# Batch 0's queries in the quadrant layout, with the head's and the units' steps in a new order: pooled attention and an MLP mixer on one core

## The chip, the core and the metric

One core of a Trainium2 chip. The time is device microseconds of one launch; the median of three runs of the kernel before is 266.4 us (266.19 to 267.63). A profile of one execution, with every instruction's start and duration and every DMA packet, stands beside the times. PE is the matrix engine (TensorE), PEld its weight loads, DVE the vector engine, ACT the scalar engine, POOL GpSimd, SP SyncE.

## What is computed

For 8 batches, 8 heads, 576 rows and head dimension 64, keys and values are averaged over groups of 8 rows (72 pooled keys), attention is taken against them, and the result goes through two MLPs, one over rows, one over channels:

```python
k_p = k.reshape(B, H, 72, 8, 64).mean(axis=3); v_p = v.reshape(B, H, 72, 8, 64).mean(axis=3)
attn = softmax(q @ k_p.T / 8)                    # 576 x 72 for each batch and head
x = (attn @ v_p), heads side by side             # 576 x 512 for each batch
h = relu(x.T @ w_tok1) @ w_tok2                  # w_tok1 576 x 256, w_tok2 256 x 576
u = x + h.T
out = u + relu(u @ w_ch1) @ w_ch2                # w_ch1 512 x 1536, w_ch2 1536 x 512
```

## The kernel before

**Units.** The channel MLP makes the bulk of the work. It runs as nine units, one for each batch's first 512 rows and a last one for all batches' remaining rows. A unit (`unit_fast`) is twelve first-layer tiles (`l1_tile`, L517: four 128x512 matmuls each, then a ReLU on ACT, L521) and seven products of the second layer (`product`, L583), which work on sums and differences of halves that DVE makes (`g_sums`, L545 and L557). A unit yields after every half tile; at each yield index the table `PLAN[n]` names the steps of other batches that are issued there. So while unit n runs, the attention of batch n+1 is done between its matmuls, and loads and poolings of batches further ahead.

**Steps.** `b.lk`, `b.lq`, `b.lv` load a batch's keys, queries, values (POOL issues these DMAs, which also cast to bf16). `b.K0`, `b.K1`, `b.V0`, `b.V1` pool the keys or values of four heads on POOL (three adds, L174, L175, then L178 or L180); a small letter (`2.v1`) puts the same on DVE; `kpool`, `vpool` do it on PE with eight identity matmuls (L253, L264). `kpT` transposes pooled keys on PE (L222) and ACT copies them to `kD`. `Q0`, `Q1` (`qD`, L284) transpose queries on DVE in 32x32 blocks of pairs, so that four heads stand in four quadrants of 32 partitions. `s0` to `s2` (`scores`, L297) multiply quadrant by quadrant (each matmul uses 32 rows of the array, the four heads four different ones) and ACT takes the exponential (L306). `av` (L379) multiplies with the values, DVE divides (L383, L384); `at` (L393) and `u` (L415) are the row MLP; `t` (L424) transposes the sum on PE; for batches 3 to 7 `M` and `T` do that by way of DRAM and DVE. `=1` to `=4` are `g_sums`, `w0` to `w3` (`weight_sum`) the same for weights, once. `g` is a gate: a one-element write on DVE and a read of it on POOL (L712, L713), which holds POOL until DVE has come that far.

**The order.** Inside `manual_schedule` every engine's instructions stand in the order in which the program issues them. Loads by POOL go through one queue in issue order, with eight transfers outstanding: issue n waits until transfer n-8 has landed.

**The head.** Before unit 0, the string `HEAD` lists the steps of batch 0, which has routes of its own. `LkA`, `LkB`, `LkT` load its keys in three parts (heads 0 to 3 and 4 to 7 of rows' groups 0 to 63, then groups 64 to 71 of all heads); `LvA`, `LvB`, `LvT` the same of values; `Lq` half the queries, the other half comes by two SP loads in fp32 that `c0` (ACT) and `c1` (DVE) cast (L690). `Lt1`, `Lt2`, `Lc1a` to `Lc1d`, `Lc2a` to `Lc2c` load weights, `Lk1`, `Lq1`, `Lv1` batch 1. `dN` issues N matmuls on a zeroed tile (L679, `warm`), whose result nobody reads. `q0` to `q3` (`qT`, L275) transpose pairs of heads on PE, five 128x128 blocks each, and DVE copies them (L277). `kp0` to `kp2` pool the keys on PE (L232), DVE copies into `kpz`, which has zeroes beside each head; `kt0` to `kt2` (L243) transpose that so that even and odd rows of queries have each a zero-padded key tile `kT`. `o0` to `o3`, `e0` to `e3` (`score`, L318) are eight scores of two heads each, every one with one exponential on ACT (L322). `a00` to `a14` (`avh`, L333), `m00` to `m14` (`ath`, L356), `X0` to `X3` and `A0` to `A3` (`uT_x`, L468; `uT_a`, L476) are the rest of attention and the row MLP for four heads at a time; `p0`, `p1` reorder `w_tok2` on ACT and POOL (L159). Score tiles and `a` tiles share two double banks of PSUM in turn (`ps_two`); other products take turns in four single banks.

Of the kernel before, what the change touches and what calls it, by code (L numbers as in the profile page):

```python
# [20 lines left out]
HEAD = """LkA LkT LkB LvT Lq LvA LvB Lt1 Lk1 Lt2 Lc1b Lc1a Lq1 Lc1c Lv1 Lc1d p1 Lc2a Lc2b Lc2c d2 d2 d3 d1 d4 d4 c0 c1 prep q0 kp0 kp1 kt0 q1 d1 o0 kt1 kp2 e0 e1 q3 kt2 o1 q2 e3 vpool0 o3 e2 a00 vpool1 a02 o2 m01 d1 d1 m00 a04 X1 m03 a14 m02 X0 m04 p0 a10 a12 1.kpool m10 m14 m12 m13 m11 A1 A0 X2 X3 A2 A3"""  # L21
PLAN = [
# [13 lines left out]
def kernel(  # L36
# [21 lines left out]
    NE = (BR + 1) // 2  # L58
    EV, OD = NE * BP, (BR - NE) * BP
# [43 lines left out]
    kpz = area[0:SP, 0:1536].rearrange("j (h e d) -> j h e d", h=H, e=3)  # L103
    kT = area[:, 2048:2048 + 2 * H * SP].rearrange("m (o k) -> m o k", o=2)
    qT0 = area[:, 3200:3200 + 2 * HP * EV].rearrange("m (a l n) -> m a l n", a=HP, l=2)
# [30 lines left out]
    def q_pairs(a0, a1):  # L136
        return q[0, 2 * a0:2 * a1].rearrange("(a l) (p r) d -> (l p) a (r d)", l=2, r=BR)
# [49 lines left out]
    def batch_steps(b):  # L187
# [5 lines left out]
        def prepare():  # L193
            kp = att.tile([SP, 2, 2, 4, D // 2], BF16, name="kp") if b >= 1 else None
            st.update(kp=kp, vp=values[par], ex=exps[par], xt=rests[b // 2 % 2])
            if not first:
                st["kD"] = att.tile([P, 2, 2, SP], BF16, name="kD")
# [29 lines left out]
        def kp2(h0, h1):  # L227
            def go():
                ps = take([P, 512], FP32)
                n = (h1 - h0) * D  # L230
                for i in range(POOL):
                    nc.tensor.matmul(out=ps[0:SP, 0:n], lhsT=ident[0:SP, 0:SP], rhs=loaded[b, "k"][:, h0:h1, i, :],  # L232
                                     start=(i == 0), stop=(i == POOL - 1))
                nc.vector.tensor_copy(out=kpz[:, h0:h1, 1, :], in_=ps[0:SP, 0:n].rearrange("j (h d) -> j h d", d=D))
                give(ps)
            return go

        def kt2(h0, h1):
            def go():
                ps = take([P, 2, h1 - h0, SP], BF16)  # L240
                for odd in range(2):
                    for h in range(h0, h1):
                        nc.tensor.transpose(out=ps[:, odd, h - h0, :],  # L243
                                            in_=kpz[:, h, 1 - odd:3 - odd].rearrange("j e d -> j (e d)"),
                                            identity=ident[0:SP, 0:SP])
                nc.vector.tensor_copy(out=kT[:, :, h0 * SP:h1 * SP], in_=ps.rearrange("m o h j -> m o (h j)"))
                give(ps)
            return go
# [22 lines left out]
        def qT(hp):  # L271
            def go():
                ps = take([P, NE, 2, BP], BF16)
                for rr in range(NE):
                    nc.tensor.transpose(out=ps[:, rr].rearrange("m l p -> m (l p)"),  # L275
                                        in_=loaded[b, "q"][:, hp, rr * P:(rr + 1) * P], identity=ident)
                nc.vector.tensor_copy(out=qT0[:, hp].rearrange("m l (r p) -> m r l p", p=BP), in_=ps)  # L277
                give(ps)
            return go

# [8 lines left out]
        def scores(i):  # L289
            def go():  # L290
                pss = [ps_two.tile([P, 2, 512], FP32, name="p2") for _ in range(2)]
                spans = [(i, 0, 0, S1)] if i < 2 else [(g, g * (S - S1), S1, S) for g in range(2)]
                for g, o, n0, n1 in spans:
                    for db in range(2):
                        for l in range(4):
                            quad = slice(l * 32, (l + 1) * 32)
                            nc.tensor.matmul(out=pss[l // 2][0:SP, l % 2, o:o + n1 - n0], lhsT=st["kD"][quad, g, db, :],  # L297
                                             rhs=st["qD"][quad, g, n0:n1, db], start=(db == 0 and o == 0),
                                             stop=(db == 1), tile_position=(l * 32, 0), skip_group_check=True)
                exv = st["ex"][:, 0:H * S].rearrange("j (g a l n) -> j a l g n", g=2, a=2, l=2)  # L300
                for a in range(2):
                    if i < 2:
                        dst, src = exv[:, a, :, i, 0:S1], pss[a][0:SP, :, 0:S1]
                    else:
                        dst, src = exv[:, a, :, :, S1:S], pss[a][0:SP, :, 0:2 * (S - S1)].rearrange("j l (g n) -> j l g n", g=2)
                    nc.scalar.activation(out=dst, in_=src, func=AF.Exp, scale=scale)  # L306
            return go

        def score(hp, odd):
            n = OD if odd else EV  # L310

            def go():
                ps = ps_two.tile([P, 2, 512], FP32, name="p2")
                exv = st["ex"][:, 0:H * S].rearrange("j (h n) -> j h n", h=H)[:, 2 * hp:2 * hp + 2]
                for hl in range(2):
                    h = 2 * hp + hl
                    keys = slice(h * SP, (h + 1) * SP)
                    nc.tensor.matmul(out=ps[0:SP, hl, 0:n], lhsT=kT[:, odd, keys], rhs=qT0[:, hp, hl, 0:n],  # L318
                                     start=True, stop=True)
                dst = exv.rearrange("j h (r p) -> j h r p", p=BP)[:, :, odd:BR:2, :]  # L320
# [462 lines left out]
```

## Time and profile before

| | |
|---|---|
| median of three runs | 266.4 us (266.19, 266.4, 267.63) |
| span of the profiled execution | 264.4 us, from first to last instruction; the runs' median is 2.0 us longer |
| PE busy | 256.2 us (97%), 2121 matmuls |
| DVE, ACT, POOL busy | 178.4 us (67%), 119.6 us (45%), 153.1 us (58%) |
| PE's first matmul, first key matmul, first L517 | 1.19, 8.04 and 24.60 us |
| DMA rate from 16 to 57.5 us | 199 to 206 GB/s |

PE's longest waits by the list of waits are 1.3 us for the first keys and 0.9 us for pooled keys of batch 2 (at 57 us); everything else is under half a microsecond. From about 15 us on the matmuls follow one another almost without a hole.

### The profile page before, as it was taken

What the parts mean: (1) busy time and instruction counts of PE and PEld (TensorE: products, weight loads), DVE (VectorE), ACT (ScalarE), POOL (GpSimd) and SP (SyncE); (2) the same over time, 40 slices, a digit from 0 to 9 for tenths busy, and PEclk for the clock granted to TensorE, in tenths of its full rate; (3) what the DMA queues carried; (4) which work ended last, traced back from release to release, by engine and by line L of the source; (5) the groups of instructions that cost most, each with busy time, mean ns of one, the idle gap of its engine ahead of it and who ended that gap; (6) DMA issues with size and microseconds to landing.
All of it is one profiled execution on the core that took longest, in us unless ns stands there. A gap on an engine that the chain in (4) does not pass through costs nothing.

```text
span 264.4 us, 5328 instructions
## 1 busy us (share of the span) xinstructions
PE 256.2 (97%) x2121; PEld 160.3 (61%) x2121; DVE 178.4 (67%) x370; ACT 119.6 (45%) x195; POOL 153.1 (58%) x177
## 2 busy tenths in 40 slices
PE   8799999989999999999999999999999999999994
PEld 3685466744677545774487447744874486486483
DVE  3557569996787655895599678844795576184183
ACT  2355763149536456425641575165435412612700
POOL 8577326899999999988959982898200010100000
PEclk9999999999999999999999999999999999999999
DMA  6999999993088928699447940830513053404104
GB/s 141 193 195 206 205 207 208 205 216 80 4 129 141 166 82 171 149 202 266 91 132 107 232 144 17 158 94 4 159 38 122 30 170 80 121 0 102 59 0 159
DMA packets 31704, 34.29 MB, mean 130 GB/s; under 512 B 3136, under 2 KB 23744, under 8 KB 31680
## 3 DMA queue, kind: packets, MB, share of 16 engines
q0 software_dynamic: 17632, 17.64, 42.3%
q1 hardware_dynamic: 13632, 15.93, 20.2%
q10 hardware_dynamic: 416, 0.39, 0.5%
q8 instruction: 16, 0.26, 0.4%
q14 instruction: 8, 0.07, 0.1%
HBM read 38.99 MB, written 12.58 MB: 195 GB/s over the span
## 4 chain that ended last, share of the span: by engine, by line
PE 73%; DVE 12%; POOL 8%; issue 3%; DMA 2%; ACT 1%; POOLq 0%; ACTq 0%
PE p1c L517 10%; PE p1b L517 8%; PE p1a L517 7%; PE p1d L517 7%; PE p1d L583 6%; PE p1c L583 5%; PE p1b L583 4%; PE p1a L583 4%; POOL t L174 3%; PE p L297 3%; DVE x L384 3%; DVE area L545 3%; PE p L379 2%; DMA kr<-in_k_dram 2%; POOL t L175 2%
## 5 line engine op out<-in xcount | busy, mean ns | idle before, releaser
L517 PEld LDWEIGHTS <-w_ch 128*128 128x128 bf16 x432 | 39.5, 98 | 44.4 <-issue 2.7
L713 POOL COPY flag<-flag 1x1 f32<-1x1 f32 x47 | 15.3, 326 | 86.0 <-DVE flag L712 86.0
L583 PEld LDWEIGHTS <-area 128*128 128x128 bf16 x432 | 41.4, 98 | 7.8 <-issue 1.2
L306 ACT ACTIVATE ex<-p 72x768 bf16<-72x768 f32 x42 | 31.6, 803 | 17.1 <-PE p L297 17.1
L583 PEld LDWEIGHTS <-GT 128*128 128x128 bf16 x324 | 30.7, 98 | 7.9 <-issue 1.6
L175 POOL TENSOR_TENSOR t<-t 72x512 f32<-72x512 f32 x23 | 31.2, 1358 | 1.8
L517 PE MATMUL p1c<-uT,w_ch 128*128 128x512 bf16 x116 | 31.4, 379 | 0.0
L521 ACT ACTIVATE GT<-p1b 128x512 bf16<-128x512 f32 x27 | 16.1, 597 | 27.5 <-PE p1b L517 20.9
L521 ACT ACTIVATE GT<-p1c 128x512 bf16<-128x512 f32 x32 | 19.1, 598 | 15.5 <-PE p1c L517 11.7
L517 PE MATMUL p1b<-uT,w_ch 128*128 128x512 bf16 x96 | 26.0, 379 | 0.0
L174 POOL TENSOR_TENSOR t<-kr 72x1024 f32<-72x1024 bf16 x12 | 25.5, 2121 | 0.4
L174 POOL TENSOR_TENSOR t<-vr 72x1024 f32<-72x1024 bf16 x11 | 23.4, 2125 | 1.0 <-DMA vr<-in_v_dram 0.5
L517 PE MATMUL p1a<-uT,w_ch 128*128 128x512 bf16 x88 | 23.9, 379 | 0.0
L517 PE MATMUL p1d<-uT,w_ch 128*128 128x512 bf16 x84 | 22.2, 379 | 0.0
L521 ACT ACTIVATE GT<-p1a 128x512 bf16<-128x512 f32 x25 | 14.9, 597 | 15.4 <-PE p1a L517 14.8
L521 ACT ACTIVATE GT<-p1d 128x512 bf16<-128x512 f32 x24 | 14.4, 599 | 12.8 <-PE p1d L517 7.3
L384 DVE TENSOR_TENSOR x<-p,den 128x512 bf16<-128x512 f32 x28 | 19.3, 691 | 1.0
L545 DVE TENSOR_TENSOR area<-GT 128x1536 bf16<-128x1536 bf16 x9 | 11.3, 1257 | 11.9 <-ACT GT L521 6.7
L557 DVE TENSOR_TENSOR area<-GT 128x1536 bf16<-128x1536 bf16 x9 | 9.5, 1054 | 11.3 <-ACT GT L521 11.3
L379 PEld LDWEIGHTS <-ex 72*128 72x128 bf16 x280 | 12.9, 98 | 6.5 <-DVE x L384 1.4
L379 PE MATMUL p<-vp,ex 72*128 72x65 bf16 x280 | 14.4, 194 | 0.3 <-POOL vp L180 0.2
L118 POOL DMA_DIRECT2D kr<-in_k_dram x17 | 10.9, 646 | 5.6 <-PE p1b L222 1.9
(185 smaller groups left out, 464.2 us busy)
## 6 DMA issues: line engine op xcount, KB each, us to landing
out_dram<-o SPq DMA_DIRECT2D x32, 256.0 KB, 4.2
qb<-in_q_dram POOLq DMA_DIRECT2D x7, 576.0 KB, 9.4
kr<-in_k_dram POOLq DMA_DIRECT2D x7, 512.0 KB, 8.4
vr<-in_v_dram POOLq DMA_DIRECT2D x7, 512.0 KB, 14.0
w_ch<-in_moe_w_ch_dram POOLq DMA_DIRECT2D x5, 512.0 KB, 14.8
mem<-u SPq DMA_DIRECT2D x10, 256.0 KB, 2.2
v<-mem SPq DMA_DIRECT2D x20, 128.0 KB, 2.9
area<-in_q_dram SPq DMA_DIRECT2D x2, 288.0 KB, 3.0
```

Source lines behind the costliest of these rows:

```text
L118: nc.gpsimd.dma_start(out=t[j0:j1, h0:h1].rearrange("j h i d -> j h (i d)"), in_=src[b, h0:h1].rearrange("h (j i) d -> j h (i d)", i=POOL) ...
L174: eng.tensor_tensor(out=t4[:, 0:n], in0=t[:, hs, 0:4], in1=t[:, hs, 4:8], op=ALU.add)
L175: eng.tensor_tensor(out=t4[:, 0:n, 0:2], in0=t4[:, 0:n, 0:2], in1=t4[:, 0:n, 2:4], op=ALU.add)
L306: nc.scalar.activation(out=dst, in_=src, func=AF.Exp, scale=scale)
L379: nc.tensor.matmul(out=ps[:, h // 4, (h % 4) * (D + 1):(h % 4 + 1) * (D + 1)], lhsT=st["ex"][:, h * S + n0:h * S + n0 + P], rhs=st["vp"][: ...
L384: nc.vector.tensor_tensor(out=dst.rearrange("p (a h d) -> p a h d", a=2, d=D), in0=view[:, :, :, 0:D], in1=den[rows, :, :, None].broadcast ...
L517: nc.tensor.matmul(out=ps, lhsT=w_ch1[:, kk, m * P:(m + 1) * P], rhs=uT[kk], start=(kk == 0), stop=(kk == 3))
L521: nc.scalar.activation(out=GT[:, m, :], in_=ps, func=AF.Relu)
L545: nc.vector.tensor_tensor(out=out, in0=a, in1=b, op=ALU.subtract)
L557: nc.vector.tensor_tensor(out=S4[:, 0], in0=GT[:, f, hi], in1=GT[:, sec, hi], op=ALU.add)
L583: nc.tensor.matmul(out=ps[i] if split else ps[:, i], lhsT=chunk(u, i, a(m)), rhs=w(m), start=start and m == 0 and (i == 0 or split), stop= ...
L713: nc.gpsimd.tensor_copy(out=flag[:, 1:2], in_=flag[:, 0:1])
```

## The change

Batch 0 takes the route of the other batches. The queries are loaded in quadrant layout (`first_q`), transposed by DVE (`Q0`, `Q1`), the pooled keys go into `kp` and `kD`, and the scores use 32-row tiles: `S0` and `S1` make queries 0 to 511 of four heads each, `S2` the last 64 of all. `qT`, `score`, `kpz`, `kT` and `qT0` go, with their memsets. Each of `kp0`, `kp1` pools four heads (before: two, two, four). The remaining edits are orders: `HEAD` is a new sequence, without any `d` step, and every `PLAN[n]` is new.

```diff
-HEAD = """LkA LkT LkB LvT Lq LvA LvB Lt1 Lk1 Lt2 Lc1b Lc1a Lq1 Lc1c Lv1 Lc1d p1 Lc2a Lc2b Lc2c d2 d2 d3 d1 d4 d4 c0 c1 prep q0 kp0 kp1 kt0 q1 d1 o0 kt1 kp2 e0 e1 q3 kt2 o1 q2 e3 vpool0 o3 e2 a00 vpool1 a02 o2 m01 d1 d1 m00 a04 X1 m03 a14 m02 X0 m04 p0 a10 a12 1.kpool m10 m14 m12 m13 m11 A1 A0 X2 X3 A2 A3"""
+HEAD = """prep LvT LkT LkA Lq LkB LvA Lt1 LvB Lc1a Lt2 Lc1b Lk1 Lq1 Lv1 Lc1c Lc2a c0 Lc1d p1 c1 kp0 Q0 kt0 S0 Lc2c Lc2b kp1 Q1 kt1 S1 vpool0 a02 a00 vpool1 S2 X1 m03 a04 m01 X0 a10 m00 p0 m02 a12 m04 a14 m11 m10 X2 m13 m12 m14 A0 A1 A2 X3 A3 1.kpool 0.u1 1.Q0"""
...
-        def kt2(h0, h1):
-                ps = take([P, 2, h1 - h0, SP], BF16)
-                for odd in range(2):
-                    for h in range(h0, h1):
-                        nc.tensor.transpose(out=ps[:, odd, h - h0, :],
-                                            in_=kpz[:, h, 1 - odd:3 - odd].rearrange("j e d -> j (e d)"),
+        def kt2(g):
+                ps = take([P, 2, SP], BF16)
+                for e in range(2):
+                    nc.tensor.transpose(out=ps[:, e, :], in_=st["kp"][:, g, e].rearrange("j l d -> j (l d)"),
...
+            name[f"s{g}"], name[f"S{g}"], name[f"f{g}"] = (scores([(g, *r)]) for r in ((0, S1), (0, 512), (S1, S)))
+        name["s2"], name["S2"] = (scores([(g, n, S) for g in range(2)]) for n in (S1, 512))
...
-            nc.sync.dma_start(out=qf[:, a:a + 1, :], in_=q_pairs(a, a + 1))
+            nc.sync.dma_start(out=qf[:, a, :], in_=first_q(0)[:, a * BR * D:(a + 1) * BR * D])
```

`make_identity` (POOL) stands ahead of the fourth entry of `HEAD`: before that was `LvT`, now it is `LkA`. In the tables of the units the poolings change engines in four places: one of the two value poolings of batch 1 goes from PE to POOL (`1.V1`), and `5.k0`, `7.v0` and `7.v1` go from POOL to DVE. `2.K0` and `2.K1` stand at indices 20 and 32 of `PLAN[0]` (before 27 and 32), `2.kpT` at index 0 of `PLAN[1]` (before index 44 of `PLAN[0]`). `0.u1` moves from unit 0 into the head, and the gates stand elsewhere.

More of the change, by code (lines that the diff above doesn't have):

```diff
@@ L57 @@
     BP, BR = 64, S // 64
-    NE = (BR + 1) // 2
-    EV, OD = NE * BP, (BR - NE) * BP
     S1 = 3 * P
@@ L102 @@
     area = early.tile([P, 6 * 1024], BF16, name="area")
-    kpz = area[0:SP, 0:1536].rearrange("j (h e d) -> j h e d", h=H, e=3)
-    kT = area[:, 2048:2048 + 2 * H * SP].rearrange("m (o k) -> m o k", o=2)
-    qT0 = area[:, 3200:3200 + 2 * HP * EV].rearrange("m (a l n) -> m a l n", a=HP, l=2)
+    qf2 = area[:, 0:4 * BR * D].bitcast(FP32).rearrange("p (a n) -> p a n", a=2)
     values = [singles.tile([SP, H, D + 1], BF16, name=f"vp{i}") for i in range(2)]
@@ L134, in first_kv, with first_q @@
         kv(loaded[0, key], k if key == "k" else v, 0, h0, h1, j0, j1)
-    def q_pairs(a0, a1):
-        return q[0, 2 * a0:2 * a1].rearrange("(a l) (p r) d -> (l p) a (r d)", l=2, r=BR)
+    def first_q(g):
+        return q[0, g * HP:(g + 1) * HP].rearrange("l (j n) d -> (l j) (n d)", n=2 * BR)
     def load(key, b):
@@ L193, in prepare @@
         def prepare():
[L194 to L197, printed above, removed]
+            st["kp"] = att.tile([SP, 2, 2, 4, D // 2], BF16, name="kp")
+            st["kD"] = att.tile([P, 2, 2, SP], BF16, name="kD")
+            st.update(vp=values[par], ex=exps[par], xt=rests[b // 2 % 2])
         def late(key):
@@ L225, in kpT, with kp2 @@
             give(ps)
-        def kp2(h0, h1):
+        def kp2(g):
             def go():
                 ps = take([P, 512], FP32)
-                n = (h1 - h0) * D
+                hs = slice(g * HP, (g + 1) * HP)
                 for i in range(POOL):
-                    nc.tensor.matmul(out=ps[0:SP, 0:n], lhsT=ident[0:SP, 0:SP], rhs=loaded[b, "k"][:, h0:h1, i, :],
+                    nc.tensor.matmul(out=ps[0:SP, 0:HP * D], lhsT=ident[0:SP, 0:SP], rhs=loaded[b, "k"][:, hs, i, :],
                                      start=(i == 0), stop=(i == POOL - 1))
-                nc.vector.tensor_copy(out=kpz[:, h0:h1, 1, :], in_=ps[0:SP, 0:n].rearrange("j (h d) -> j h d", d=D))
+                nc.vector.tensor_copy(out=st["kp"][:, g].rearrange("j e l d -> j e (l d)"),
+                                      in_=ps[0:SP, 0:HP * D].rearrange("j (n e) -> j e n", e=2))
                 give(ps)
             return go
-        def kt2(h0, h1):
+        def kt2(g):
             def go():
-                ps = take([P, 2, h1 - h0, SP], BF16)
-                for odd in range(2):
-                    for h in range(h0, h1):
-                        nc.tensor.transpose(out=ps[:, odd, h - h0, :],
-                                            in_=kpz[:, h, 1 - odd:3 - odd].rearrange("j e d -> j (e d)"),
-                                            identity=ident[0:SP, 0:SP])
-                nc.vector.tensor_copy(out=kT[:, :, h0 * SP:h1 * SP], in_=ps.rearrange("m o h j -> m o (h j)"))
+                ps = take([P, 2, SP], BF16)
+                for e in range(2):
+                    nc.tensor.transpose(out=ps[:, e, :], in_=st["kp"][:, g, e].rearrange("j l d -> j (l d)"),
+                                        identity=ident[0:SP, 0:SP])
+                nc.vector.tensor_copy(out=st["kD"][:, g], in_=ps)
                 give(ps)
@@ L269, in ppool @@
             return go
[L271 to L279, printed above, removed]
         def qD(g):
@@ L287, in qD, with scores @@
             return go
-        def scores(i):
+        def scores(spans):
+            n = spans[0][2] - spans[0][1]
             def go():
                 pss = [ps_two.tile([P, 2, 512], FP32, name="p2") for _ in range(2)]
-                spans = [(i, 0, 0, S1)] if i < 2 else [(g, g * (S - S1), S1, S) for g in range(2)]
-                for g, o, n0, n1 in spans:
+                for i, (g, n0, n1) in enumerate(spans):
+                    o = i * n
                     for db in range(2):
@@ L296, in go @@
                             quad = slice(l * 32, (l + 1) * 32)
-                            nc.tensor.matmul(out=pss[l // 2][0:SP, l % 2, o:o + n1 - n0], lhsT=st["kD"][quad, g, db, :],
+                            nc.tensor.matmul(out=pss[l // 2][0:SP, l % 2, o:o + n], lhsT=st["kD"][quad, g, db, :],
                                              rhs=st["qD"][quad, g, n0:n1, db], start=(db == 0 and o == 0),
@@ L301, in go @@
                 for a in range(2):
-                    if i < 2:
-                        dst, src = exv[:, a, :, i, 0:S1], pss[a][0:SP, :, 0:S1]
+                    g, n0, n1 = spans[0]
+                    if len(spans) == 1:
+                        dst, src = exv[:, a, :, g, n0:n1], pss[a][0:SP, :, 0:n]
                     else:
-                        dst, src = exv[:, a, :, :, S1:S], pss[a][0:SP, :, 0:2 * (S - S1)].rearrange("j l (g n) -> j l g n", g=2)
+                        dst, src = exv[:, a, :, :, n0:n1], pss[a][0:SP, :, 0:2 * n].rearrange("j l (g n) -> j l g n", g=2)
                     nc.scalar.activation(out=dst, in_=src, func=AF.Exp, scale=scale)
[L307 to L320, printed above, removed]
-                src = ps[0:SP, :, 0:n].rearrange("j h (r p) -> j h r p", p=BP)
-                nc.scalar.activation(out=dst, in_=src, func=AF.Exp, scale=scale)
             return go
@@ L487, in batch_steps @@
                 name[t + str(g)] = pool(nc.vector, t, g)
-        for hp in range(HP):
-            if hp < 3:
-                hs = ((0, 2), (2, 4), (4, 8))[hp]
-                name[f"kp{hp}"], name[f"kt{hp}"] = kp2(*hs), kt2(*hs)
-            name[f"q{hp}"], name[f"o{hp}"], name[f"e{hp}"] = qT(hp), score(hp, 1), score(hp, 0)
-        for i in range(3):
-            name[f"s{i}"] = scores(i)
+        for g in range(2):
+            name[f"kp{g}"], name[f"kt{g}"] = kp2(g), kt2(g)
+            name[f"s{g}"], name[f"S{g}"], name[f"f{g}"] = (scores([(g, *r)]) for r in ((0, S1), (0, 512), (S1, S)))
+        name["s2"], name["S2"] = (scores([(g, n, S) for g in range(2)]) for n in (S1, 512))
         for c in range(5):
@@ L688, in head @@
         elif s[0] == "c":
-            a = int(s[1:])
-            (nc.vector.tensor_copy if a % 2 else nc.scalar.copy)(out=loaded[0, "q"][:, a, 0:BR * D], in_=qf[:, a, :])
+            g, a = divmod(int(s[1:]), 2)
+            (nc.vector.tensor_copy if a % 2 else nc.scalar.copy)(
+                out=quarters(loaded[0, "q"])[:, g, a * BR * D:(a + 1) * BR * D], in_=(qf2 if g else qf)[:, a, :])
         else:
@@ L695, in late_q, with late_q2 @@
     def late_q():
-        nc.gpsimd.dma_start(out=loaded[0, "q"][:, 2:HP, 0:BR * D], in_=q_pairs(2, HP))
-    early_loads = {"q": late_q, "t1": load_tok1, "t2": load_tok2, }
+        nc.gpsimd.dma_start(out=quarters(loaded[0, "q"])[:, 1], in_=first_q(1))
+    def late_q2(a):
+        (nc.scalar if a == 2 else nc.sync).dma_start(out=qf2[:, a % 2], in_=first_q(1)[:, a % 2 * BR * D:(a % 2 + 1) * BR * D])
+    early_loads = {"q": late_q, "h2": lambda: late_q2(2), "h3": lambda: late_q2(3),  "t1": load_tok1, "t2": load_tok2, }
     for key in "kv":
@@ L737 @@
         for a in range(2):
-            nc.sync.dma_start(out=qf[:, a:a + 1, :], in_=q_pairs(a, a + 1))
-        qb = loaded[0, "q"] = raw.tile([P, HP, BR * D + D], BF16, name="qb")
-        nc.vector.memset(qb[:, :, BR * D:], 0.0)
-        nc.vector.memset(kpz, 0.0)
+            nc.sync.dma_start(out=qf[:, a, :], in_=first_q(0)[:, a * BR * D:(a + 1) * BR * D])
+        loaded[0, "q"] = raw.tile([P, HP, BR * D + D], BF16, name="qb")
         nc.vector.memset(w_tok1[:, 4:6, :], 0.0)
@@ L750 @@
             head(s)
-        for n in range(B + 1):
-            unit(n, PLAN[n])
+        for n, at in enumerate(PLAN):
+            unit(n, at)
 _INS = ['q', 'k', 'v', 'moe_w_tok1', 'moe_w_tok2', 'moe_w_ch1', 'moe_w_ch2']
```

18 rows, old and new, of the table PLAN are left out of this document.

## The prediction

> **What bounds the kernel now.** I read the page first, then the timeline of the first 30 us, the list of waits and the chain of waits.
>
> ```profile
> PE 256.2 (97%) x2121; PEld 160.3 (61%) x2121; DVE 178.4 (67%) x370; ACT 119.6 (45%) x195; POOL 153.1 (58%) x177
> ```
>
> PE has work for 97% of the span. So time is gained only by less work on PE or by fewer holes in it. The timeline shows where holes are (start, length, engine, line, tiles, count, idle before):
>
> ```profile
> 2.87 1.49 PE L679 MATMUL p1c<-area 128*128 128x512 bf16 x3
> ...
> 4.57 1.03 PE L679 MATMUL p1a<-area 128*128 128x512 bf16 x4
> ...
> 8.04 0.61 PE L232 MATMUL p1d<-kr,ident 72*72 72x128 bf16 x8 [1.30 <-DMA kr<-in_k_dram]
> ...
> 10.19 0.59 ACT L322 ACTIVATE ex<-p 72x512 bf16<-72x512 f32 x1 [5.86 <-PE p L318]
> ...
> 17.05 0.59 ACT L322 ACTIVATE ex<-p 72x512 bf16<-72x512 f32 x1 [0.19 <-PE p L318]
> ...
> 24.60 0.59 PE L517 MATMUL p1c<-uT,w_ch 128*128 128x512 bf16 x2
> 26.30 1.42 DVE L284 STREAM_TRANSPOSE qD<-qb 128x576 uint32<-128x576 uint32 x2
> 28.71 0.53 PE L297 MATMUL p<-qD,kD 32*72 32x384 bf16 x8
> ```
>
> The reader is to see: the warm-up matmuls go at 0.43 us each at first and at 0.22 us from 4.57 us on, 3.4 us after the first (1.19). Keys arrive, and useful work starts at 8.04; the eight scores' exponentials run from 10.19 to 17.64, and unit 0 starts at 24.60. Between 8.04 and 24.60 the work on PE, counted by its starts, is 15.4 us, so only 1.2 us of holes: small steps (`q`, `kt`, `d1`, single scores) fill each other's waits. Later there is one large hole: batch 2's pooled keys are late from POOL.
>
> ```profile
> 56.61 0.84 POOL L178 TENSOR_TENSOR kp<-t 72x256 bf16<-72x256 f32 x1
> ...
> 57.50 0.24 PE L222 MATMUL p1c<-ident,kp 72*128 72x72 bf16 x2 [0.92 <-POOL kp L178]
> ```
>
> It costs 1.08 us from start to start. All such holes from 24.6 us on sum to 2.9 us: this one, 0.37 us at 86.3 us for pooled values, 0.46 us in the last unit, the rest waits for DVE below 0.4 us.
>
> **What leaves PE.** `qT`: 20 matmuls by 0.056 = 1.1 us. `kt`: 16 become 4, by 0.032 = 0.4. Scores: 8 by 0.109 and 8 by 0.136 = 2.0 become two groups of 512 columns and one of 2 x 64; a group of eight with 384 columns takes 0.46 in the chain, where four at a time would need 0.32, so 0.14 is fill; that gives 0.57 + 0.57 + 0.25 = 1.4, a saving of 0.6. Three filler `d1`: 0.65. Together 2.7 us in the head; counted step by step from the same rows the head's work is 15.4 before and 13.0 after, and I use these. The 16 warm-ups lie ahead of 8.04 and cost nothing there. In unit 0 `1.V1` on POOL takes eight matmuls of 0.11 = 0.88 off PE. `0.u1` (0.43) only moves into the head, which then holds 13.4.
>
> **When that work can run.** The new chain, step by step; hand-offs between engines are 0.04 to 0.1 us in the timeline.
> - First keys. `LkA` stood first in POOL's queue (issue at 1.24, landing 5.4 later by the tile's view); now it is behind two 64 KB tails (0.7 each) and the identity (0.5), issue about 3.1. Its packets then find a running stream. Bounds for `kp0`: 7.9 (only bytes count) to 8.7 (5.4 again); I take 8.3, nearer the stream.
> - `kp0`: eight matmuls of 256 columns. No warm-up ran, so I take the first rows' rate: 0.21 each, 1.7, plus 0.2 latency: 10.2. DVE copies (L234, 256 columns, 0.42): 10.65. Next in DVE's order is `Q0` (0.75), and behind it the copy of `kt0` (0.24 by the slope of L246's 0.31 and 0.45), though PE has `kt0` done before: 11.7. `S0` starts at 11.7 and holds PE 1.0 at half rate.
> - `kp1` from 12.7: 0.88 at full rate, 1.71 at half; I take 1.3, since 4.4 us after its first matmul, with holes of 0.5 and 0.7, PE may or may not be released. Then copy 0.42, `Q1` 0.75, copy 0.24: `S1` at 15.7.
> - An exponential of 1024 columns: rows of 512, 640 and 768 (0.59, 0.70, 0.80) give 1.0, two in 1.9. `S1`'s end at about 18.3. `vpool0` hides beside them; `a02` 17.9, `a00` must wait for the second bank, 18.3; its division (0.21 + 0.69) ends after `a02`'s at 20.2. Only then has `S2` its second bank: 20.2, exponentials to 21.3. `a04` needs these. In the kernel before the last exponential ended at 17.64.
> - From there PE has 7.3 us, with 0.8 us of waits: `m11`, `X2`, `m14` each follow a DVE division (0.93, 0.93, 0.63) of `a10`, `a12`, `a14`. Unit 0 starts at 29.4 (24.60 before). 21.1 us for 13.4 us of work: 7.7 us of holes and half rate, where 1.2 were.
>
> Transfers are no limit in this: `Lk1` has 800 KB more ahead of it, 4.0 us at 203 GB/s, so it lands at 22.9 and `1.kpool` comes later than that; `Lc1d` lands 2.6 us later (512 KB of `Lc2a` ahead), about 36.5, and is used from 40 on. `Lt2` lands earlier, since `Lk1` is behind it; `p1` on POOL waits behind three issues, ends at about 21.8 and is needed from 25.
>
> **What the later start gives back.** POOL's poolings follow the loads, which keep their times. `2.K1` is issued with fewer gates ahead and its keys land as before (44.9): two poolings of 2.1 + 1.36 + 0.89 and one pair of issues end at about 55, unit 1 begins near 60. So the 1.08 us go, and the 0.37 us at 86.3, also POOL's. The three poolings moved to DVE cost it 1.52 + 1.64 + 0.84 = 4.0 each (the row of `2.v1`). `5.k0` must end before `5.kpT`: from index 8 to 15 PE has 5.6 us, DVE 4.75 with `Q0`. Nothing, or up to 0.5 if DVE is behind; `Q1` is queued behind it and is needed later. `7.v0`, `7.v1` fall where DVE is 40% to 70% busy: nothing, the bound the same. Other holes stay in my sum; a new order can remove them (-1.5) or double them (+1.5).
>
> **Sum.** 29.4 - 24.6 = +4.8; `0.u1` is in it (-0.43); `1.V1` -0.88; holes -1.08 - 0.37. That is +2.0: span 266.4. The profiled span is 264.4 and the runs' median 2.0 above it, so 268.4.
>
> **A rule beside the row.** The row gives the release of the clock after 3.4 us without a hole; the granted clock in the page shows nothing of it (9 throughout). The Trainium skill ("TensorE: Matmul & The Clock Gate", Part 1) says the array idles at half clock and is released after a busy window of about 3.4 us, free-running. The trace agrees on both figures. By the rule read strictly, a window with holes may not count, and the second rival would be the forecast; by the row alone the sum stands.
>
> **Rivals.**
> - *Full clock from the start, or nearly.* `kp0`, `S0` and half of `kp1` lose 0.85, 0.43 and 0.4: unit 0 at 27.7, 266.7 us. For: the release is not explained by this trace. Against: its first eight matmuls.
> - *Half clock until the chain is through.* PE is busy some two thirds of this stretch. If it stays at half rate until `vpool1` ends, add 0.4, 0.43 (`S1`), 0.88, 0.27 and 0.88 = 2.9: 271.3 us.
> - *Transfers, not the chain, set the head* (faster). If the waits I add up overlap, removed work counts in full, and the last thing unit 0 waits for is batch 1's keys: 22.9, `1.kpool` 1.73, `0.u1` 0.43, so 25.1, 264.1 us. For: PE was the bound throughout. Against: copy, transpose and copy stand in one order on DVE, and PE has nothing else in between. It decides if unit 0 starts before 26.1.
> - That the new scores are not done four at a time is excluded: L297 shows it for the same form.
>
> **Numbers.** Forecast 0.49, own range 267.2 to 269.8 by the bounds of `kp0` and the holes; full clock 0.22, half clock 0.14, transfers 0.15. Differences below 0.5% (1.33 us) a measurement can't tell from no change: 265.07 to 267.73. Slower: 0.42 of the forecast, the half clock, 0.04 of the full: 0.60. Same: the rest of both, 0.25. Faster: 0.15. The range 264.1 to 270.8 leaves out half of the fastest case and most of the half clock.
>
> **What would show it.** Right: `S0` near 11.7, `S1` near 15.7, first matmul of unit 0 near 29.4, no hole before `2.kpT`. The 256-column matmuls of `kp0` start 0.21 apart if the clock is at half, 0.11 if not. Wrong: unit 0 before 26.1, or a hole of over 1 us after 30 us (then the new tables cost, not the head).

## The result, and the profile after

The changed kernel takes 284.03 us (283.35 to 285.5, four runs), the kernel before 266.29 us beside it: a ratio of 1.0667, with a 95% interval of 1.0629 to 1.0705, so 17.7 us slower. The forecast was 268.4 us, within 264.1 to 270.8. The sign was right, the size was not. The profiled execution is the one of 285.5 us, 1.5 above the median, so its stages add up to more than 17.7 us.

The page of the kernel after (first row: busy time by engine; then PE's share and the granted clock in 40 slices):

```profile
PE 256.6 (90%) x2045; PEld 159.5 (56%) x2070; DVE 190.9 (67%) x361; ACT 118.2 (42%) x193; POOL 141.2 (50%) x160
PE   0779999639999999998889889999999999999994
PEclk9999999957999999999999999999999999999999
```

PE does 51 matmuls fewer, counted by the weight loads (2070 against 2121; 25 records of matmuls are missing in this trace), and is busy as long as before (256.6 against 256.2 us): many ran at half rate. In the page of before PE falls under 70% only in the last slice, and the clock nowhere. Here PE is at 60 and 30% in slices 8 and 9 (49.6 to 63.8 us), and the granted clock at 0.5 and 0.7 in slices 9 and 10 (56.7 to 70.9).

The timeline of the kernel after, in the head (start, length, engine, line, tiles, count, idle before):

```profile
8.09 1.89 PE L227 MATMUL p1a<-kr,ident 72*72 72x256 bf16 x8 [8.09 <-DMA kr<-in_k_dram]
...
11.30 1.07 PE L283 MATMUL p<-qD,kD 32*72 32x512 bf16 x8 [0.50 <-DVE kD L240]
...
12.30 1.92 PE L227 MATMUL p1c<-kr,ident 72*72 72x256 bf16 x8
...
15.54 1.07 PE L283 MATMUL p<-qD,kD 32*72 32x512 bf16 x8 [0.50 <-DVE kD L240]
16.54 1.92 PE L258 MATMUL p1a<-vr,ident 72*72 72x256 bf16 x8
...
22.18 0.65 ACT L293 ACTIVATE ex<-p 72x256 bf16<-72x256 f32 x2
...
32.09 0.38 PE L485 MATMUL p1d<-uT,w_ch 128*128 128x512 bf16 x1
```

`kp0` (8.09), `kp1` (12.30) and `vpool0` (16.54) go at the same 0.21 us for each 256-column matmul: the clock is at half from 8.09 on, and by the starts of later rows it stays there to about 26.8. The exponentials end at 22.8, unit 0 starts at 32.09 (24.60 before).

The same view from 47 us on, VectorE and POOL between the matmuls. (L513 and L525 are the sums `g_sums` and `weight_sum`; L170, L171, L174 the three adds of a pooling.)

```profile
47.99 3.08 DVE L513 TENSOR_TENSOR area<-w_ch 128x1536 bf16<-128x1536 bf16 x1
48.12 2.13 POOL L170 TENSOR_TENSOR t<-kr 72x1024 f32<-72x1024 bf16 x1
...
54.45 3.45 DVE L513 TENSOR_TENSOR area<-area,GT 128x1536 bf16<-128x1536 bf16 x1
54.95 2.13 POOL L170 TENSOR_TENSOR t<-kr 72x1024 f32<-72x1024 bf16 x1
57.16 1.87 POOL L171 TENSOR_TENSOR t<-t 72x512 f32<-72x512 f32 x1
57.82 0.68 DVE L594 TENSOR_TENSOR s<-p1c,u 128x512 f32<-128x512 f32 x1
...
58.55 1.01 PE L551 MATMUL p1c<-area,area 128*128 128x256 bf16 x4 [4.00 <-DVE s L594]
```

A sum takes 0.95 us when nothing is beside it; here it takes 3.08 and 3.45, and each ends 0.83 us after the POOL add that runs beside it (50.25 to 51.08; 57.08 to 57.90). PE waits 4.00 us for what stands behind the second. PE's longest waits behind the first keys, from the list of waits of the kernel after (total, times, longest):

```profile
PE p1c L551 <- DVE s L594: 4.4, 3, 4.0
PE p1a L386 <- DVE u L387: 2.5, 1, 2.5
PE p1b L217 <- DVE kp L174: 1.7, 1, 1.7
```

And the table by stages, with the granted clock (stretch, its length, busy time and count of each engine, clock, DMA share, GB/s):

```profile
8.09:26.80 18.71, 16.16 (x129) 10.91 (x130) 6.88 (x18) 6.44 (x9) 11.52 (x16) 1.00 1.24 194
...
58.50:67.80 9.30, 6.54 (x29) 4.06 (x30) 8.21 (x10) 0.02 (x1) 8.83 (x7) 0.50 0.08 12
```

After the hole PE runs 9.3 us at a granted clock of 0.50. The head's half rate the table doesn't show (1.00): the trace's first record of the clock begins at 26.9 us, and for the time ahead of it the table prints 1.00. Only the spacing of the matmuls shows the half rate.

So the two profiles (spans 264.4 and 283.7) differ by 7.5 us before unit 0 starts (24.60 to 32.09), 7.5 us in unit 0 (it takes 33.0 and 40.4; unit 1 starts at 57.58 and 72.53) and 4.3 us behind it.

### The profile page after: what moved, and what is told of

Its sections match the earlier page's. It is cut to its first block, busy times and chain, and to the rows that moved or that the text cites. A ratio compares the mean times of both kernels' runs of the same rounds, so it can differ in the third digit from the quotient of the medians.

```text
span 283.7 us, 5175 instructions
## 1 busy us (share of the span) xinstructions
PE 256.6 (90%) x2045; PEld 159.5 (56%) x2070; DVE 190.9 (67%) x361; ACT 118.2 (42%) x193; POOL 141.2 (50%) x160
## 4 chain that ended last, share of the span: by engine, by line
PE 66%; DVE 15%; DMA 10%; issue 5%; SPq 2%; POOL 1%; ACT 0%; DVEq 0%; ACTq 0%; POOLq 0%
PE p1c L485 7%; PE p1a L485 7%; PE p1b L485 7%; PE p1d L485 7%; DMA v<-mem 6%; PE p1b L551 5%; PE p1d L551 5%; DVE area L513 4%; PE p1a L551 4%; PE p L283 4%; PE p1c L551 3%; PE p L350 2%; DMA mem<-u 2%; SPq L417 2%; DMA kr<-in_k_dram 2%
## 5 line engine op out<-in xcount | busy, mean ns | idle before, releaser
L685 POOL COPY flag<-flag 1x1 f32<-1x1 f32 x36 | 9.7, 268 | 101.3 <-DVE flag L684 101.3
L293 ACT ACTIVATE ex<-p 72x768 bf16<-72x768 f32 (+2 forms) x48 | 36.0, 802 | 28.7 <-PE p L283 28.7
L171 POOL TENSOR_TENSOR t<-t 72x512 f32<-72x512 f32 x21 | 29.8, 1421 | 1.7
L489 ACT ACTIVATE GT<-p1d 128x512 bf16<-128x512 f32 x28 | 16.7, 596 | 29.8 <-PE p1d L485 19.7
L485 PE MATMUL p1c<-uT,w_ch 128*128 128x512 bf16 x96 | 26.3, 379 | 1.2 <-DVE uT L429 1.0
L485 PE MATMUL p1d<-uT,w_ch 128*128 128x512 bf16 x95 | 26.9, 379 | 0.4 <-issue 0.2
L489 ACT ACTIVATE GT<-p1a 128x512 bf16<-128x512 f32 x26 | 15.5, 597 | 19.8 <-PE p1a L485 19.1
L170 POOL TENSOR_TENSOR t<-kr 72x1024 f32<-72x1024 bf16 x11 | 23.5, 2134 | 0.4
L489 ACT ACTIVATE GT<-p1c 128x512 bf16<-128x512 f32 x28 | 16.8, 598 | 13.6 <-PE p1c L485 8.0
L170 POOL TENSOR_TENSOR t<-vr 72x1024 f32<-72x1024 bf16 x10 | 21.9, 2185 | 0.4
L525 DVE TENSOR_TENSOR area<-GT 128x1536 bf16<-128x1536 bf16 x9 | 10.1, 1120 | 13.5 <-ACT GT L489 13.5
L283 PE MATMUL p<-qD,kD 32*72 32x384 bf16 (+3 forms) x256 | 13.8, 312 | 1.0 <-DVE kD L240 1.0
L551 PE MATMUL p1c<-area,area 128*128 128x256 bf16 x72 | 10.6, 296 | 4.0 <-DVE s L594 4.0
```

The lines of the kernel that those rows point to most:

```text
L170: eng.tensor_tensor(out=t4[:, 0:n], in0=t[:, hs, 0:4], in1=t[:, hs, 4:8], op=ALU.add)
L171: eng.tensor_tensor(out=t4[:, 0:n, 0:2], in0=t4[:, 0:n, 0:2], in1=t4[:, 0:n, 2:4], op=ALU.add)
L283: nc.tensor.matmul(out=pss[l // 2][0:SP, l % 2, o:o + n], lhsT=st["kD"][quad, g, db, :], rhs=st["qD"][quad, g, n0:n1, db], start=(db == 0 ...
L485: nc.tensor.matmul(out=ps, lhsT=w_ch1[:, kk, m * P:(m + 1) * P], rhs=uT[kk], start=(kk == 0), stop=(kk == 3))
L489: nc.scalar.activation(out=GT[:, m, :], in_=ps, func=AF.Relu)
L525: nc.vector.tensor_tensor(out=S4[:, 0], in0=GT[:, f, hi], in1=GT[:, sec, hi], op=ALU.add)
```

## The experiments

Each line of edits is against the kernel named; times are medians with their range.

**Head and tables apart.** First the new head with the old tables, then the reverse.

```diff
 # after, with
-PLAN: after          HEAD: "... A3 1.kpool 0.u1 1.Q0"
+PLAN: before         HEAD: "... A3 1.kpool"
```

> The new head (without its last two steps) with the old tables of the units. Theory 'two costs' (the head runs at half clock and starts unit 0 some 7 us late; and apart from that the new tables put POOL's poolings on top of DVE's sums): unit 0 starts at 31 to 32 us, 1536-wide sums in unit 0 take 0.95 to 1.7 us again, no hole over 1.5 us in the units, 271 to 275 us. Rival 'late start alone' (the tables are harmless, the units' holes come from the late head): holes of 3 us and more in unit 0 stay, 280 us or more.

Measured: 273.63 us (273.49 to 273.73), ratio 1.0274 (1.0241 to 1.0307); unit 0 starts at 31.75. So the head alone costs 7.3 us. From unit 0's start to the end the profile has 271.7 - 31.75 = 239.95 us, the kernel before 264.4 - 24.60 = 239.8: the later start gave nothing back. The hole ahead of `2.kpT` is still there, 1.25 us at 63.6: its poolings are held by gates and come later with the unit.

```diff
 # before, with
-PLAN: before         HEAD: "... A2 A3"
+PLAN: after          HEAD: "... A2 A3 0.u1 1.Q0"
```

> The old head (with 0.u1 and 1.Q0 at its end) with the new tables of the units. Theory 'two costs': unit 0 starts near 25 us, 2.K0 meets the sums of unit 0 because its keys land near 45 us and no gate holds it, some of the 1536-wide sums take 2 to 3.5 us, 270 to 276 us. Rival 'late start alone': sums at 0.95 to 1.3 us, 265 to 267 us.

Measured: 270.44 us (269.97 to 272.16), ratio 1.0167 (1.012 to 1.0213). From its list of waits:

```profile
PE p1d L415 <- DVE u L416: 2.1, 1, 2.1
PE p1b L222 <- DVE kp L178: 1.5, 1, 1.5
```

Of the three waits of the kernel after, the one of 4.0 us for `s` isn't there; the one for `u` (L415 here, L386 there) is 2.1 us instead of 2.5 and ends at 51.3 us, again behind two held sums (2.28 and 2.01 us); the one for `kp` is that of `5.kpT`. A new one of 1.0 us, ending at 37.0, is for the values that `1.V1` pools. So the tables alone cost 4.1 us; 7.3 + 4.1 = 11.4, and 6.3 of the 17.7 us come only when both are together.

**The head's clock.** Sixteen warm-up matmuls ahead of `kp0`.

```diff
 # after, HEAD
-... c1 kp0 Q0 kt0 S0 ...
+... c1 d2 d2 d3 d1 d4 d4 kp0 Q0 kt0 S0 ...
```

> The kernel after with the 16 warm-up matmuls ahead of kp0, as before had them. If half clock is what makes the head late: kp0's matmuls 0.11 us apart, unit 0 at 27.5 to 29 us (32.1 without), time 3 to 5 us less than after, 279 to 281. Rival 'the chain of hand-offs makes it late whatever the clock': unit 0 less than 1.5 us earlier.

Measured: 287.81 us (284.78 to 289.69): no gain, against my theory. Its runs spread too far for an interval. Its stages:

```profile
8.10:13.40 5.30, 3.28 (x28) 1.99 (x28) 1.99 (x5) 1.93 (x2) 2.54 (x5) 0.95 1.22 179
13.40:22.90 9.50, 8.48 (x82) 6.18 (x82) 3.17 (x9) 4.08 (x6) 7.42 (x11) 0.50 1.30 204
```

The first keys ran at full rate; but with PE busy 3.28 of 5.30 us (62%) the clock went back to half, by the record at 12.8 us (hence 0.95 in the first row) and for 10.2 us. Unit 0 started at 29.78, 2.3 us earlier than in the kernel after, and the sums of unit 0 met the adds again (holes of 4.16 and 3.05 us). What ate the 2.3 us and more lies for the most part in unit 2, which is 3.4 us longer than in the kernel after: a hole of 2.86 us at 125.4, in which VectorE waits for a tile that comes back from DRAM (L429), and the clock at half behind it from 128.9 to 132.3 us. What made that tile late I did not settle.

So the next one, on the kernel of e1, also filled the holes (17 fillers, beside the 16 ahead of `kp0`).

```diff
 # e1, HEAD
-... c1 kp0 Q0 kt0 S0 Lc2c Lc2b kp1 Q1 kt1 S1 vpool0 a02 a00 vpool1 S2 X1 m03 a04 ...
+... c1 d2 d2 d3 d1 d4 d4 kp0 d2 Q0 kt0 d2 S0 Lc2c Lc2b kp1 d2 Q1 kt1 d2 S1 vpool0 d2 a02 a00 vpool1 d3 S2 d2 X1 m03 d1 a04 ... m02 d1 a12 ...
```

> The new head with the old tables (273.6 us), and warm-up matmuls ahead of kp0 plus short fillers in the gaps of the chain up to a12, 16 + 17 matmuls. If the half clock is most of the head's loss: all of the head's matmuls at full rate, unit 0 at 27.3 to 28.5 us (31.75 without), 269.5 to 270.5 us. Rival 'hand-offs alone': unit 0 after 30 us, 272 or more.

Measured: 269.6 us (269.21 to 269.64), ratio 1.0127 (1.0095 to 1.0158). In its timeline everything is at full rate:

```profile
8.46 1.04 PE L227 MATMUL p1c<-kr,ident 72*72 72x256 bf16 x8 [1.37 <-DMA kr<-in_k_dram]
...
14.42 0.65 PE L283 MATMUL p<-qD,kD 32*72 32x512 bf16 x8 [0.34 <-DVE kD L240]
```

Unit 0 starts at 27.73. So 4.0 of the head's 7.3 us (273.63 - 269.6) are the half clock. The other 3.3 I put down to the chain of hand-offs between the engines; no run takes it apart, and what the fillers themselves cost is in it. The unit starts 3.1 us later than before (27.73 - 24.60), 2.7 of them counted from the first keys (8.46 here, 8.04 before), though PE has less work of its own.

**POOL's adds and VectorE's sums.** One step moved by seven indices, behind the weight sum `w3`, and a gate `g` put ahead of it. (The run has both; what each does alone is not measured.)

```diff
 # after, PLAN[0]
-20: "3.lv 2.K0 1.av3", ... 27: "w3", 28: "1.u2", 32: "2.K1"
+20: "3.lv 1.av3", ... 27: "w3 g 2.K0", 28: "1.u2", 32: "2.K1"
```

> The kernel after with one step moved: 2.K0 from index 20 of the first table to index 27, behind the sums of unit 0 and a gate. Theory 'POOL's poolings hold DVE's sums up': the sums of unit 0 take 0.95 to 1.3 us, the holes at 54, 59 and 62 us (4.2, 2.8, 0.6) go and the half clock after them too, 273 to 278 us. Rival 'late start alone': the same holes, 282 us or more.

Measured: 275.32 us (274.97 to 275.76), ratio 1.0339 (1.0304 to 1.0374): 8.7 us less than the kernel after. The tile view of the sums between 24 and 75 us (duration in ns, smallest, middle, largest, then first and last start), first of the kernel after:

```profile
L513 DVE TENSOR_TENSOR area<-w_ch x2: 2234/2660/3085, 48.0 to 66.3; 128x1536 bf16<-128x1536 bf16 x2
...
L513 DVE TENSOR_TENSOR area<-area,GT x1: 3452/3452/3452, 54.4 to 54.4; 128x1536 bf16<-128x1536 bf16 x1
```

then of this kernel:

```profile
L513 DVE TENSOR_TENSOR area<-w_ch x2: 948/951/954, 47.5 to 57.0; 128x1536 bf16<-128x1536 bf16 x2
...
L513 DVE TENSOR_TENSOR area<-area,GT x1: 955/955/955, 50.1 to 50.1; 128x1536 bf16<-128x1536 bf16 x1
```

The sums are back at 0.95 us and PE's clock is at full speed throughout. But for the gate the work is the same, only the adds start at 53.66 instead of 48.12.

The reverse, on the kernel before: every gate `g` removed.

```diff
 # before, every PLAN[n]
-8: "g", 9: "0.u3 1.s1", ... 18: "1.av4 g", ... 26: "1.at0 g", 27: "2.K0", ...
+9: "0.u3 1.s1", ... 18: "1.av4", ... 26: "1.at0", 27: "2.K0", ...
```

> The kernel before without any gate: POOL's poolings start as soon as their data are there. Theory 'POOL's adds hold DVE's two-input sums up': 1536-wide sums of 1.6 to 3.5 us in the stretches where a pooling runs, holes on PE behind them, 270 to 285 us. Rival 'gates only hold POOL back': sums stay at 0.95, the hole at 56 us (1.08) goes, 264.5 to 266.5 us.

Measured: 276.45 us (275.28 to 280.13), ratio 1.0372 (1.0315 to 1.0429), with unit 0 at 23.98. Its timeline before a hole of 2.0 us at 145.6:

```profile
140.72 2.11 POOL L174 TENSOR_TENSOR t<-vr 72x1024 f32<-72x1024 bf16 x1
140.84 2.81 DVE L545 TENSOR_TENSOR area<-area,GT 128x1536 bf16<-128x1536 bf16 x1
...
142.91 1.86 POOL L175 TENSOR_TENSOR t<-t 72x512 f32<-72x512 f32 x1
...
143.68 1.91 DVE L545 TENSOR_TENSOR area<-GT,area 128x1536 bf16<-128x1536 bf16 x1
...
147.75 0.43 PE L379 MATMUL p<-vp,ex 72*128 72x65 bf16 x8 [1.86 <-DVE x L384]
```

The same hold (2.81 and 1.91 us) in tables that the change has not touched, and PE waits for a division (L384) that is queued behind the two. The largest hole, 5.08 us at 113.4, ends with VectorE's wait for a tile that comes back from DRAM (L458); what made that late I did not follow. The gates are worth some 10 us to the kernel before (276.45 - 266.2; 8.4 to 11.4 by the interval). How much of it is the hold alone this run doesn't say, since it has that largest hole too.

**`5.k0`.** On the kernel of e4, back from VectorE to POOL.

```diff
 # e4, PLAN[3]
-5: "4.av3 g", ... 10: "5.k0 4.at0 5.Q1"
+5: "4.av3 5.K0 g", ... 10: "4.at0 5.Q1"
```

> As the run with 2.K0 behind the sums, and 5.k0 back from DVE to POOL, at its old index 5. If the DVE pooling is what 5.kpT waits for (hole of 1.9 us at 130.7 us there): that hole goes, 1.5 to 2.3 us less than that run's 275.3, 273 to 274 us. Rival 'it is late for another reason': within 0.5 us of 275.3.

Measured: 274.67 us (274.15 to 274.87), so 0.65 less, where 1.5 to 2.3 were expected; the intervals of the two ratios overlap (1.0284 to 1.035 here, 1.0304 to 1.0374 in e4), so it may be nothing. From its list of waits:

```profile
PE p L350 <- POOL vp L176: 1.4, 1, 1.4
PE p1b L217 <- POOL kp L174: 0.6, 1, 0.6
```

The wait of 1.7 us for `kp` is gone (0.6 are those of `2.kpT`, as in e4); POOL has one pooling more ahead of batch 5's values, and PE waits 1.4 us for these instead.

**The quadrant layout in the old order of the head.** Loads nearly in the sequence of before (`Lq` comes earlier), `Q0` early, `1.kpool` in the middle, fillers in the holes, the tables of before.

```diff
 # e6, HEAD
-prep LvT LkT LkA Lq LkB LvA ... kp0 d2 Q0 kt0 d2 S0 ... kp1 d2 Q1 kt1 d2 S1 ... A2 X3 A3 1.kpool
+prep LkA LkT Lq LkB LvT LvA ... Q0 ... kp0 d2 kt0 d1 S0 Q1 d1 kp1 d2 kt1 d1 S1 vpool0 vpool1 S2 a02 a00 d2 a12 ... a04 1.kpool a14 p0 m12 m13 m11 m10 m04 X2 m14 X3 A0 A1 A2 A3
```

> Quadrant layout of batch 0's queries with loads in the old sequence (values behind keys, batch 1's keys early), Q0 ahead of the keys on DVE, warm-ups and fillers, both value poolings ahead of the attention products, batch 1's key pooling in the middle, and the old tables. If the order and the clock, not the layout, cost the time: unit 0 at 24 to 26 us, 265 to 268 us. Rival 'the layout itself is slower in the head': unit 0 later than 27.5, over 269 us.

Measured: 269.71 us (268.77 to 272.23), ratio 1.0165 (1.0104 to 1.0227), unit 0 at 27.46: no better than e6. In its timeline:

```profile
23.98 0.38 PE L439 MATMUL p1c<-ident,x 128*128 128x128 bf16 x4 [0.68 <-ACT AT L333]
...
25.52 0.38 PE L439 MATMUL p1b<-ident,x 128*128 128x128 bf16 x4 [0.93 <-DVE AT L336]
```

`X2` and `X3` take a single bank of PSUM that a tile `at` still holds. The next one gave these banks back first, and moved `2.kpT` later, nearly as the change does (the tables' edit is that of e10, below).

```diff
 # e7, HEAD
-... 1.kpool a14 p0 m12 m13 m11 m10 m04 X2 m14 X3 A0 A1 A2 A3
+... 1.kpool m04 a14 p0 m12 m13 m11 m10 A0 A1 m14 X2 X3 A2 A3
```

> The kernel after with the kernel before's tables and the head of e7_head_in_old_order, whose tail is rearranged so that m04, m14, A0 and A1 come before X2 and X3 (the four single banks of PSUM are then free when X2 and X3 want one); in the tables 2.kpT moves from index 44 of unit 0 to index 1 of unit 1, and 2.s0 from 1 to 3 (time for POOL's adds to end). Theory 'held banks' (X2 and X3 waited 0.68 and 0.93 us for a free bank, after a hole of 0.81): unit 0 near 25.4 instead of 27.5, the hole at 2.kpT gone (-1.1): 269.7 - 2.1 - 1.1 = 266.5 us, level with the kernel before. Rival 'DVE's chain sets the tail, the banks only showed it': unit 0 stays within 0.5 us of 27.5, and 268.3 us. If the quadrant layout could pay in work (2.3 us of PE less in the head), 264 to 265 would show; I don't expect it.

Measured: 269.21 us (267.68 to 270.48), ratio 1.0104 (1.0065 to 1.0144), unit 0 at 27.56. The waits for banks are gone. Unit 0 starts where it did, but the two profiles can't be compared by that alone: here the first keys came at 8.48 us, in e7 at 7.34, and every row up to `1.kpool` (19.38 and 20.52) is later by these 1.14 us. (In the five profiles with the head of before the first keys came between 7.37 and 8.25, so such a difference is nothing unusual.) Counted from the first keys the head takes 19.08 us instead of 20.12: the new order of the tail was worth 1.0 us, where the theory of the banks wanted 2.1, and for the rest the rival stands (the chain over VectorE and ACT). The times (269.21 and 269.71) are too near each other to show it. With the keys of e7 this order would start unit 0 at about 26.4 (an estimate: 7.34 + 19.08). No order that I ran started it before 27.4; that none exists is not shown.

**Two parts of the tables, alone, on the kernel before.** First `2.kpT` later:

```diff
 # before, PLAN[0] and PLAN[1]
-44: "g 2.kpT 2.Q1 3.Q0"     1: "2.v1 2.s0"
+44: "g 2.Q1 3.Q0"           1: "2.kpT 2.v1", 3: "2.s0"
```

> The kernel before with one step moved, as the change does it: 2.kpT from index 44 of unit 0 to index 1 of unit 1, and 2.s0 from 1 to 3. Theory (the hole is 1.08 us because PE asks for the keys too early, and nothing else waits there): 1.08 less, 265.2 us. Rival (the scores and divisions behind 2.kpT become late instead): 266.0 to 266.5, with a new hole of 0.5 to 1 us in unit 1.

Measured: 266.13 us (265.52 to 266.6, 12 runs) beside 266.3, ratio 0.9986 (0.9967 to 1.0005): no difference. The hole of 1.08 us is gone and PE's wait for batch 3's values grew. From its list of waits:

```profile
PE p L379 <- POOL vp L180: 0.9, 1, 0.9
```

In the profile of before that wait was 0.2 us. By the matmuls' starts the hole there (85.7 us) is 1.10 us against 0.37: 0.74 of the 1.08 us comes back at POOL's next due step.

Then, with this, `1.V1` on POOL in the place of `1.vpool1` on PE.

```diff
 # e10, PLAN[0]
-8: "g", 9: "0.u3 1.s1", 10: "1.vpool1 2.lv", 12: "1.s2 1.vpool0"
+8: "g", 9: "1.V1 0.u3 1.s1", 10: "1.vpool0 2.lv", 12: "1.s2"
```

> e10_before_kpT_later with one more part of the change: the values of batch 1, heads 4 to 7, are pooled on POOL (1.V1, behind the gate at index 8 of unit 0) instead of PE (1.vpool1). PE does 0.88 us less. Theory of the change's tables: 265.2 - 0.9 = 264.3 us. Rival from e4 and e8 (POOL's adds hold DVE's two-input sums): the adds run from about 33 to 37.5 us, the first sum (=3, at 36.1) is held by 1 to 1.5 us, and the keys and values of batch 2, whose loads POOL issues behind the adds, come up to 4 us later: 265.0 to 266.5.

Measured: 268.32 us (266.82 to 270.55, 12 runs), ratio 1.0082 (1.0051 to 1.0113): 2 us slower than before. Its timeline:

```profile
37.74 0.55 PE L379 MATMUL p<-vp,ex 72*128 72x65 bf16 x12 [2.23 <-POOL vp L180]
```

PE saves 0.88 us and waits 2.23 for the values. The profile is 0.9 us longer than that of e10 (spans 265.5 and 264.6); what makes the median 2.2 us longer than e10's it doesn't show in full. (In the change the unit runs 7 us later, and this wait isn't there.)

**Both causes together.** The kernel after with the fillers of e6 and the moved `2.K0` of e4.

```diff
 # after: HEAD and PLAN[0]
-... c1 kp0 Q0 kt0 S0 ...                       20: "3.lv 2.K0 1.av3", ... 27: "w3"
+... c1 d2 d2 d3 d1 d4 d4 kp0 d2 Q0 kt0 d2 S0 ...    20: "3.lv 1.av3", ... 27: "w3 g 2.K0"
```

> The kernel after with two things together: 2.K0 behind the weight sums as in e4_K0_behind_sums, and the 16 warm-up matmuls and fillers in the head's holes as in e6_head_kept_warm. Theory (the two causes are separate: half clock in the head 4.0 us, POOL's adds on the sums 8.7 us): 284.0 - 8.7 - 4.0 = 271.3 us, unit 0 near 28. Rival from e3_warm, where unit 0 began 2.3 us earlier and the time was not less (the units are held by POOL's chain of loads and adds, so an earlier head is lost as holes later): 274 to 275.5, with new holes of 2 us or more in sum behind unit 0.

Measured: 271.86 us (271.12 to 272.69), ratio 1.0201 (1.0147 to 1.0256), unit 0 at 27.98; 271.3 was the theory's number, 274 or more the rival's. The two causes add: 12.2 us go, of 8.7 + 4.0. What is left against before is 5.4 us: the head's chain (3.3) and 2.1 us of the tables, in which the hole ahead of `5.kpT` (1.90 us) stands as in the kernel after.

No kernel here beats the kernel before by more than a measurement can tell.

## Why the prediction was wrong, step by step

- **First keys, half rate, first scores: right.** `kp0` 8.3, measured 8.09; its matmuls 0.21 apart, as forecast; `S0` 11.7 and 11.30; `S1` 15.7 and 15.54.
- **The clock's release in `kp1`: mis-sized.** I took 1.3 us for `kp1`, half of it released. It took 1.92, and the release came at 26.9. The head that resulted is the rival "half clock until the chain is through": unit 0 at 29.4 + 2.9 = 32.3, measured 32.09. I gave it 0.14. e6 prices the half clock at 4.0 us. PE was busy 16.16 of 18.71 us in this stretch, in rows with holes of 0.5 us, and for most of it that did not release the clock.
- **A rule beside this row.** The Trainium skill ("TensorE: Matmul & The Clock Gate", Part 1) says a busy window of about 3.4 us releases the clock and an idle one takes it back, and that these windows run freely. The traces agree with an uninterrupted 3.4 us (the warm-ups of before), and the stretches between two changes of the granted clock are 3.41 us long or whole multiples of it (in e3 6.83, 10.24, 34.13, 6.83 us and so on). But what took the clock back in e3 was no idle window: in the two steps of 3.41 us ahead of the loss at 12.8 us PE was busy 63 and 59%, and behind the first keys (8.44) it never waited longer than 0.56 us. How busy a window has to be, no run here measures. At the same place 60 and 77% (e6) and 48 and 84% (e12) kept the clock; on the way up, in the kernel after, steps of 70, 70 and 85% at half rate did not release it, and it came behind two that were full.
- **"What the later start gives back": the step that failed.** I wrote that `2.K1` is issued "with fewer gates ahead", its poolings end at about 55, and holes of 1.08 and 0.37 us go. e1 shows that the later start gives back nothing by itself, and e10 that the 1.08 us, once taken out, come back to two thirds at POOL's next step. I read the gates as a delay only. They keep POOL's adds off VectorE's sums: without a gate between them the adds of `2.K0` began at 48.12, right behind the loads of `3.lv` (the keys had been there since 46.2), and the sums at 47.99, since the late head had pushed them to that very place. In the kernel before the adds began at nearly the same time, but behind the gate and the last sum, which ended at 47.86:

```profile
46.91 0.95 DVE L545 TENSOR_TENSOR area<-w_ch,area 128x1536 bf16<-128x1536 bf16 x1
...
47.08 0.83 POOL L713 COPY flag<-flag 1x1 f32<-1x1 f32 x1 [0.83 <-DVE flag L712]
...
47.87 2.11 POOL L174 TENSOR_TENSOR t<-kr 72x1024 f32<-72x1024 bf16 x1
```

Forecast: -1.45; measured: +8.7 (e4). This is most of the 15.6 us by which I was off: 10.2, beside 2.5 of the head (7.3 instead of 4.8) and 1.9 ahead of `5.kpT`. In e2, with the head on time, the wait of 4.0 us wasn't there and the clock was not lost; that fits the 6.3 us that head and tables cost more together than apart.
- **A rule that I did not weigh.** The Trainium skill ("SBUF — State Buffer", "Who interferes with whom") says that a VectorE instruction with two inputs in SBUF and a GpSimd instruction that reads SBUF exclude each other on a shared port, for a whole instruction. The traces agree: the sums, which read two tiles in SBUF, are held (0.95 to 3.45 us), and beside the same adds L594 and L387, with one input in PSUM, keep their 0.68 to 0.74. The Trainium skill also says there that the order of issue decides who blocks. By the recorded starts the sum came first at 47.99 and at 54.45, by 0.13 and 0.50 us, and lost; at 151.69 it came first by 0.72 and kept its 0.95. Whether a record starts before the port is asked for, no run here shows.
- **`5.k0`, "nothing, or up to 0.5": mis-sized.** The hole ahead of `5.kpT` is 1.91 us. Its first add took 3.83 us on VectorE, not 1.52, with a POOL add of 2.11 beside it, again two engines on SBUF. From the timeline of the kernel after:

```profile
136.28 3.83 DVE L170 TENSOR_TENSOR t<-kr 72x1024 f32<-72x1024 bf16 x1
...
136.93 2.11 POOL L170 TENSOR_TENSOR t<-vr 72x1024 f32<-72x1024 bf16 x1
```

- **`1.V1`, -0.88 in the sum: not shown.** On the kernel before it cost 2.2 us (e11 against e10). In the change the values are not waited for, so the 0.88 may have come; no run takes it out there.
- **Transfers set the head (faster): fell.** Batch 1's keys were there at 22.9, as forecast, and unit 0 began 9 us later; with full clock and nearly the old sequence of loads (e9) it still began at 27.56, 19.1 us behind its first keys.
- **The sign of "wrong" that I named did show:** a hole of over 1 us behind 30 us, "then the new tables cost, not the head". It was both: 7.3 of the head, 8.7 of one step in the tables that only the late head makes so dear, 1.7 of the rest.

## What to carry to other kernels

Before a step on POOL is moved or its gate taken away, list which VectorE instructions with two SBUF inputs will run beside it, and price each meeting at the length of the POOL instruction, not at its own; a gate that looks like a delay may be the only thing that keeps the two apart. A shift of the whole program by some microseconds (here a late head) can make such meetings where there were none, so a shift has to be checked against everything whose time is fixed by transfers. And a stretch of small matmuls with half-microsecond holes is priced at half rate until a trace shows otherwise; fillers without use are work that can pay.

## What the runs showed of the hardware that I had not expected

- How regular the hold is: in the kernel after, 12 of 40 sums are held, and each ends 0.81 to 0.83 us after the end of a POOL add, whatever its own start. Their time over 0.95 us sums to 11.0 us; in the profile of before it is 4.8 (6 sums), in e4 2.3 (5 sums), in e8 14.7 (11 sums). An add that follows on such a sum is longer too: 1.87 instead of 1.27 us (L171), 1.43 instead of 0.84 (L174). POOL's DMA issues beside a sum cost it nothing (0.95 us).
- One hole (PE's wait of 4.0 us) was dear twice: PE then ran at a granted clock of 0.50 from 58.5 to 67.8 us, though it worked 6.54 of these 9.3 us.
- The table shows a granted clock of 1.00 in a stretch (8.09 to 26.8 us of the kernel after) where the spacing of the matmuls, 0.21 us for 256 columns, says half; later in the same trace it shows 0.50 for the same spacing. The trace's first record of the clock begins at 26.9 us, so the 1.00 ahead of it rests on none. There the spacing is what can be relied on.
